# Uncast pixels, GpSimd adds and paired key jobs for the second batch of a spatial-reduction attention and GELU kernel

## The chip, the core and the metric

The kernel runs on one core of one Trainium2 chip. The metric is the device time of one launch in microseconds, the median of several runs; lower is better. The core has TensorE for matrix products (PE in the profile), ScalarE for activation functions (ACT), VectorE for elementwise work (DVE), GpSimd (POOL), and SyncE (SP), which here only issues transfers. Transfers run on 16 DMA engines. Products land in PSUM, which has eight banks of 128 x 512 float32.

## The reference

Two stages follow one another. Four batches of queries attend to keys that are a 4 x 4 average of an image, projected by one matrix; keys and values are the same. The result, 49152 rows of 128, goes through a feed-forward block of width 2048 with a sigmoid approximation of GELU.

```python
B, C, Hh, Ww = (4, 128, 384, 32)       # q: (4, 12288, 128), kv: (4, 384, 32, 128)
...
kv_pool = kv.reshape(B, H // r, r, W // r, r, C).mean(axis=(2, 4))   # r = 4
kv_flat = kv_pool.reshape(B, -1, C) @ w_sr                           # 768 keys a batch
k = v = kv_flat
s = scale * (q @ k.transpose(0, 2, 1))
s = s - s.max(-1, keepdims=True)
a = np.exp(s)
a /= a.sum(-1, keepdims=True) + 1e-09
return (a @ v).astype(np.float32)
...
h = x @ w_in                                                         # 128 -> 2048
g = h * (1.0 / (1.0 + np.exp(-1.702 * h)))
return (g @ w_out).astype(np.float32)                                # 2048 -> 128
```

## The kernel before

The work is cut into 96 groups of 512 rows. In attention a group has 6 chunks (128 keys by 512 rows), in the feed-forward block 16 chunks (128 hidden units by 512 rows). The program runs in two rounds: attention of groups 0 to 47, feed-forward of the same groups, then both again for groups 48 to 95. A Python scheduler in the kernel decides the order of all instructions while the program is built; each engine then takes its own instructions in that order.

One step of the main pipeline makes up to three chunks at once. TensorE fills three banks, and ScalarE turns them into bf16 in SBUF with one instruction, while the other three banks are filled:

```python
def fill_attn(chunks, ps):
    for k, (i, jc) in enumerate(chunks):
        rhs = qTs[i // 4][:, 0, (i % 4) * G:(i % 4 + 1) * G]
        nc.tensor.matmul(ps[:, k, :], kTs[i // GB][:, jc * 128:(jc + 1) * 128], rhs, start=True, stop=True)
    nc.scalar.activation(place([("a",) + c for c in chunks]), ps, AF.Exp, scale=scale)
...
def fill_moe(chunks, ps):
    ...
    nc.scalar.activation(place([("m",) + c for c in chunks]), ps, AF.Gelu_apprx_sigmoid)
```

Two banks (6 and 7) are left for everything else: the sums of values, the pooling, the keys. `acc()` hands them out in turn. A sum of values collects three tiles of 128 rows in one bank; VectorE then divides and writes the result to `x`, and the bank is free again:

```python
def drain_attn(t, a):
    ...
        nc.tensor.matmul(av_of[u][:, k * (C + 1):(k + 1) * (C + 1)], weights(("a", i, jc))[:, o:o + T],
                         vs[i // GB][:, jc, 0:C + 1], ...)
    ...
        nc.vector.reciprocal(rec, ps[:, :, C])
        ...
        nc.vector.tensor_tensor(to, ps[:, :, 0:C], rec.unsqueeze(2).broadcast_to([128, TS, C]), MUL)
```

The pixels of a batch are six chunks of 128 image half-rows. Those of the first two batches are loaded by a transfer that GpSimd issues and that turns float32 into bf16 on the way. TensorE adds four neighbours in a row by accumulating four products, and four neighbouring rows by its second operand `sum4`. A later job makes the keys and values of this chunk:

```python
def load_chunk(b, jc):
    a, ch = divmod(jc, HC)
    t = x_tile(XS - 1 - jc)
    nc.gpsimd.dma_start(out=t, in_=kv_r[b, a, ch])
    kv_tiles[b, jc] = t.rearrange("p (wp w1 c) -> p w1 wp c", w1=r, c=C)

def pool_chunk(b, jc):
    ps = acc()
    t = kv_tiles.pop((b, jc))
    for wp in range(4):
        for w in range(r):
            nc.tensor.matmul(ps[:, 32 * wp:32 * wp + 32], t[:, w, wp, :], sum4,
                             start=(w == 0), stop=(w == r - 1))
    pTs[b, jc] = kvtmp.tile([128, 128], BF, name="pTc", bufs=2)
    nc.vector.tensor_copy(pTs[b, jc], ps[:, 0:128])
...
def key_and_value(b, jc):
    ...
    nc.tensor.matmul(ps[:, 0:128], w_sr_sb, pTs[b, jc], start=True, stop=True)
    nc.tensor.matmul(ps[:, 128:256], pTs.pop((b, jc)), w_sr_sb, start=True, stop=True)
    nc.vector.tensor_copy(kTs[b][:, jc * 128:jc * 128 + 128], ps[:, 0:128])
    nc.vector.tensor_copy(vs[b][:, jc, 0:C], ps[:, 128:256])
```

`background(i)` starts the side work when group `i` of the attention begins. A gate (a one-element memset on VectorE, then one on GpSimd that waits for it) holds GpSimd's transfers back to that point; VectorE itself does not wait there:

```python
def background(i):
    ...
    if i in CAST:            # CAST = {0: [5], 13: [6], 14: [7], 15: [8], ...}: queries to bf16 in DRAM
        gate()
        for s in CAST[i]:
            cast_q(s)
    if i in (10, 12):
        gate()
        for jc in range(i % 10 * 3 // 2, i % 10 * 3 // 2 + 3):
            load_chunk(1, jc)
    if 0 <= i - 16 < JC:
        extras.append((key_and_value, 1, i - 16))
    if 0 <= i - 15 < JC:
        extras.append((pool_chunk, 1, i - 15))
```

Batch 1 is used from group 24 on. Some chunks are not ScalarE's: `early` and `rolling` exponentials and `lent` GELU chunks are made by VectorE with polynomials, a step at a time between its other work. A lent GELU chunk takes 15 VectorE instructions, two of them reciprocals of half a chunk.

Of the kernel before, what the change touches and what calls it, by code (L numbers as in the profile page):

```python
# [24 lines left out]
def kernel(  # L25
    ctx, tc, q, kv, w_sr, moe_w_in, moe_w_out, out,
):
    nc = tc.nc
    B, N, C = q.shape
    _, H, W, _ = kv.shape  # L30
    r = 4
    Hp, Wp = H // r, W // r
    J = Hp * Wp
    JC = J // 128
    d_ff = moe_w_in.shape[1]
    FCH = d_ff // 128
    scale = 1.0 / (C ** 0.5)
    G = 512
    SG = 4 * G
    NG = B * N // G  # L40
    NS = NG // 4
    GB = NG // B
# [10 lines left out]
    kv_r = kv.rearrange("b (ch p) (a w) c -> b a ch p (w c)", p=128, a=2)  # L53
# [6 lines left out]
    XS = NS // R  # L60
# [7 lines left out]
    kvtmp = ctx.enter_context(tc.tile_pool(name="kvtmp", bufs=1))  # L68
# [3 lines left out]
    opool = ctx.enter_context(tc.tile_pool(name="op", bufs=3))  # L72
# [43 lines left out]
    HC = H // 128  # L116
    h = J // 2
    kv_tiles, kv_sums, pooled, pTs, kTs, vs = {}, {}, {}, {}, {}, {}

    def new_keys(b):  # L120
        kTs[b] = kvres.tile([128, J], BF, name="kT")

        vs[b] = kvres.tile([128, JC, C + 8], BF, name="v")
        nc.vector.memset(vs[b][:, :, C:C + 1], 1.0)
# [16 lines left out]
        pTs[b, jc] = kvtmp.tile([128, 128], BF, name="pTc", bufs=2)  # L141
        nc.vector.tensor_copy(pTs[b, jc], ps[:, 0:128])

    def key_chunk(b, jc):
        if jc == 0:
            new_keys(b)
# [8 lines left out]
        vs[b, jc] = True  # L155

    def key_and_value(b, jc):
        if (b, jc) == (1, 0):
            new_keys(b)
        ps = acc()  # L160
        nc.tensor.matmul(ps[:, 0:128], w_sr_sb, pTs[b, jc], start=True, stop=True)
        nc.tensor.matmul(ps[:, 128:256], pTs.pop((b, jc)), w_sr_sb, start=True, stop=True)
        nc.vector.tensor_copy(kTs[b][:, jc * 128:jc * 128 + 128], ps[:, 0:128])  # L163
        nc.vector.tensor_copy(vs[b][:, jc, 0:C], ps[:, 128:256])
        vs[b, jc] = True
# [103 lines left out]
    for m in range(0, 128, 32):  # L269
        p = slice(m, m + 32)  # L270
# [3 lines left out]
    sum4 = cpool.tile([128, 32], BF)  # L274
# [3 lines left out]
    w_sr_sb = cpool.tile([128, C], BF)  # L278
# [40 lines left out]

    early = range(NG // R, NG // R + EARLY)  # L320
    rolling = [(i, JC - 1) for i in [*range(38, NG // R, 6), *range(57, 90, 6)]]
    lent = [(g, FCH - 1) for g in range(52, 94, 3)]
    aside = agpool.tile([128, K, 512], BF, name="aside")

    def weights(c):
# [112 lines left out]
    def lent_gelu(ps, out):  # L438
# [23 lines left out]
        for m in (0, 256):  # L462
            nc.vector.reciprocal(b[:, m:m + 256], a[:, m:m + 256])  # L463
            yield RECIPROCAL
        nc.vector.scalar_tensor_tensor(out, raw, -LN2 / 1.702, b, MUL, MUL)
# [21 lines left out]
    PART, FIRST = 24, 3  # L487

    def put_away(n, m):
        size = PART // 2 if n == 0 and m > FIRST else PART  # L490
        for o in range(m * PART, m * PART + PART, size):
            lo = n * XS * SG + o * T
            nc.sync.dma_start(out=x_bf[lo:lo + size * T, :].rearrange("(k p) c -> p k c", p=T),
                              in_=x[:, o * T:(o + size) * T].rearrange("p (k c) -> p k c", k=size))

    def bring_back(n, m):
        o = m * PART
        lo = n * XS * SG + o * T
        nc.sync.dma_start_transpose(out=x[:, o * T:(o + PART) * T].unsqueeze(1), in_=x_bf[lo:lo + PART * T, :])
# [6 lines left out]
    def gate():  # L506

        one = gate_tile[:, gates[0] % 8:gates[0] % 8 + 1]
        gates[0] += 1
        nc.vector.memset(one, 0.0)  # L510
        nc.gpsimd.memset(one, 0.0)  # L511

    TURN = {6: 3, 7: 4, 8: 5, 20: 6, 21: 7, 22: 8, 30: 9, 32: 10, 35: 11, 40: 12}
    CAST = {0: [5], 13: [6], 14: [7], 15: [8], 25: [9, 10], 26: [11, 12]}
    CAST_MOE = {20: 13, 21: 14, 22: 15, 23: 16, 33: 17, 34: 18, 35: 19, 36: 20, 37: 21, 38: 22, 39: 23}

    def background(i):

        first_round = i < GB * 2
        s = TURN.get(i, NS) if first_round else i // 4 + 3 if i % 4 == 0 else NS  # L520
        if s < NS:
            load_qT(s)
        if i in CAST:
            gate()
            for s in CAST[i]:
                cast_q(s)
        if i in (10, 12):
            gate()
            for jc in range(i % 10 * 3 // 2, i % 10 * 3 // 2 + 3):
                load_chunk(1, jc)  # L530
        if 0 <= i - 16 < JC:
            extras.append((key_and_value, 1, i - 16))
        if 0 <= i - 15 < JC:
            extras.append((pool_chunk, 1, i - 15))
        if i in (28, 33, 38):
            put_away(0, (i - 28) // 5)
        if i in (31, 36, 41):
            bring_back(0, (i - 31) // 5)
        if i == 27:
            gate()  # L540
            nc.gpsimd.dma_start(out=w_in_sb, in_=moe_w_in)
        if i == 28:
            gate()
            nc.gpsimd.dma_start(out=w_out_sb, in_=moe_w_out.rearrange("(o p) c -> p o c", p=128))
# [34 lines left out]
    extras = []  # L579
# [67 lines left out]
    for n in range(R):  # L647
        part = [c for c in chunks if c[0] // (NG // R) == n]
        while part:
            m = sizes.pop(0) if sizes else K  # L650
# [12 lines left out]
        while flat:  # L663
            m = K if len(flat) > sum(rest) else rest.pop(0)
# [25 lines left out]
    def jobs(p):  # L690

        nonlocal now
        for f, *args in first.get(p, ()):
            if f in COST:
                now = max(now, free[next_acc()])
            f(*args)
            if f in COST:
                now += COST[f][0]
                free[last_acc] = copied(f)

    def prepare(p):

        nonlocal now
        kind, part = seq[p]
        for i, jc in part:
            if (kind, i) not in begun:
                begun.add((kind, i))
                (background if kind == "a" else background_moe)(i)
            while kind == "a" and ((key_and_value, i // GB, jc) in extras or (transpose_q, i) in extras):
                f, *args = extras.pop(0)  # L710
                now = max(now, free[next_acc()]) + COST[f][0]
                f(*args)
                free[last_acc] = copied(f)
# [20 lines left out]


    FIXED, CHUNK, SWITCH, HANDOVER, EVACUATE = 0.295, 1.978, 6.0, 1.0, 4.5
    COST = {pool_chunk: (1.9, 2.6), key_chunk: (0.3, 2.4), value_chunk: (0.3, 2.4),
            transpose_q: (1.05, 4.2), early_fill: (1.0, 5.5), key_and_value: (0.55, 3.5),
            transpose_pooled: (0.9, 3.6), make_k: (0.8, 3.2), make_v: (0.8, 3.7)}
    COPY = {pool_chunk: 1.5, key_chunk: 1.5, value_chunk: 1.5, key_and_value: 2.8, transpose_q: 3.2}  # L740
    SMALL = 0.26
    RECIPROCAL = 10.5
    PAUSE = 4.0
    end, extra_at = [], 0.0
    source, dve = None, 0.0
# [2 lines left out]
    def on_dve(cost):  # L748
        nonlocal dve
        dve = max(dve, now + 1.0) + cost  # L750


    def copied(f):
        if f not in COPY:
            return now + COST[f][1]
        on_dve(COPY[f])
        return max(now + COST[f][1], dve)

# [28 lines left out]
    for n in range(len(seq)):  # L787
        fill(n + 2)
        jobs(n + 3)
        while True:  # L790
# [33 lines left out]
            kind, i, c = source[0]  # L824
# [58 lines left out]
```

The softmax here doesn't subtract the row's maximum and nothing guards it: scores larger than these inputs give would overflow.

## Time and profile before

| | |
|---|---|
| median of 3 runs | 950.75 us (950.52 to 951.18) |
| span of the profiled execution | 949.0 us |
| ScalarE busy | 933.9 us |
| TensorE busy | 941.5 us |
| VectorE busy | 536.8 us |
| GpSimd busy | 67.0 us |
| GELU instructions of ScalarE | 510, 682.2 us |
| exponential instructions of ScalarE | 192, 245.8 us |
| cast loads of pixels by GpSimd | 12 of 512 KB written, median 10.5 us from issue to landing |

A line of the groups names the line of the program, the engine, the operation, what is written and read with its shape, then the number of instructions; after the bar stand the busy time of the group in us, the mean ns of one instruction, and the idle time of the engine just before them with what ended most of it. A line of the timeline or of the chain of waits begins with the start in us from the start of the span and the duration in us. TensorE's matmuls are pipelined, so its busy time is not the same as its work. In the program before, L588 is the GELU, L342 the exponential, L340 the scores, L353 the sum of values, L139 the pooling, L376 and L379 the division of the attention's result, L130 the loads of pixels, and L510 the gate's memset on VectorE.

### The profile page before, as it was taken

The page shows a single profiled execution, that of the slowest core. Times are in us where ns is not written, and L with a number is a line of the kernel's source. Part 1 is how long each engine was busy: PE and PEld are TensorE (multiplying, and loading weights), DVE is VectorE, ACT ScalarE, POOL GpSimd, SP SyncE. Part 2 cuts the span into 40 slices and gives each one's busy share as a digit, 9 for nine tenths or more (in the row PEclk, how much of TensorE's full clock was granted, in tenths as well). Part 3 has the DMA queues.
Part 4 walks back from the last instruction along what each step waited for, and adds up shares of the span by engine and source line. Part 5 has one row for each costly group of instructions (what it writes and reads, how often), then busy time and mean ns, then how long its engine had stood idle before and what let it go on. Part 6 is the DMA issues. An engine that isn't in the chain of part 4 may idle for free.

```text
span 949.0 us, 15424 instructions
## 1 busy us (share of the span) xinstructions
PE 941.5 (99%) x6314; PEld 503.1 (53%) x6314; DVE 536.8 (57%) x1037; ACT 933.9 (98%) x708; POOL 67.0 (7%) x115
## 2 busy tenths in 40 slices
PE   8999999999999999999999999999999999999998
PEld 4677776444444444454446777754444444444444
DVE  5643553102477777778655765365666665566631
ACT  5999999999999999999999999999999999999998
POOL 4101001330000232000000000000000000000000
PEclk9999999999999999999999999999999999999999
DMA  9999922999867799865335583552222222222222
GB/s 182 203 181 193 214 57 42 157 127 170 162 132 113 116 147 125 123 103 78 65 55 112 133 160 77 134 122 35 44 34 45 34 46 34 45 33 45 34 45 45
DMA packets 372871, 94.93 MB, mean 100 GB/s; under 512 B 346736, under 2 KB 370416, under 8 KB 372464
## 3 DMA queue, kind: packets, MB, share of 16 engines
q1 hardware_dynamic: 343872, 61.31, 36.5%
q0 software_dynamic: 28656, 32.51, 22.6%
q8 instruction: 49, 0.80, 0.4%
q14 instruction: 22, 0.18, 0.1%
q10 hardware_dynamic: 272, 0.13, 0.0%
HBM read 52.49 MB, written 48.76 MB: 107 GB/s over the span
## 4 chain that ended last, share of the span: by engine, by line
ACT 88%; PE 9%; DMA 2%; issue 0%; DVE 0%; POOL 0%; POOLq 0%
ACT ag L588 71%; ACT ag L342 17%; PE banks L340 4%; PE banks L353 3%; DMA x<-in_kv_dram 1%; DMA qT<-q_bf 1%; PE banks L139 0%; PE banks L586 0%; PE banks L624 0%; ACT L588 0%; PE banks L596 0%; PE banks L233 0%; ACT L342 0%; DVE kT L163 0%; POOL x L222 0%
## 5 line engine op out<-in xcount | busy, mean ns | idle before, releaser
L588 ACT ACTIVATE ag<-banks 128x1536 bf16<-128x1536 f32 (+1 forms) x510 | 682.2, 1507 | 0.0
L586 PE MATMUL banks<-x,w_in_sb 128*128 128x512 bf16 x1522 | 411.7, 379 | 0.1
L596 PE MATMUL banks<-ag,w_out_sb 128*128 128x512 bf16 x1506 | 407.8, 379 | 0.0
L342 ACT ACTIVATE ag<-banks 128x1536 bf16<-128x1536 f32 (+2 forms) x192 | 245.8, 1439 | 3.7 <-PE banks L340 3.3
L596 PEld LDWEIGHTS <-w_out_sb 128*128 128x128 bf16 x1520 | 148.5, 98 | 178.0 <-issue 0.9
L586 PEld LDWEIGHTS <-w_in_sb 128*128 128x128 bf16 x1522 | 147.3, 98 | 170.4 <-issue 1.1
L607 DVE STREAM_TRANSPOSE o_sb<-banks 128x512 f32<-128x512 f32 x95 | 67.9, 715 | 210.7 <-PE banks L596 199.9
L353 PEld LDWEIGHTS <-ag 128*128 128x128 bf16 x2272 | 146.1, 98 | 46.4 <-issue 0.6
L353 PE MATMUL banks<-v,ag 128*128 128x129 bf16 x2272 | 163.7, 220 | 0.1
L340 PE MATMUL banks<-qT,kT 128*128 128x512 bf16 x544 | 148.7, 379 | 1.6 <-DVE kT L163 1.0
L432 DVE SCALAR_TENSOR_TENSOR ea<-ea,eb 128x512 f32<-128x512 f32 x128 | 87.8, 686 | 3.2
L376 DVE RECIPROCAL rec<-banks 128x3 f32<-128x3 f32 x124 | 22.2, 179 | 96.0 <-PE banks L353 96.0
L379 DVE TENSOR_TENSOR x<-banks,rec 128x384 bf16<-128x384 f32 x124 | 69.1, 557 | 4.3
L340 PEld LDWEIGHTS <-kT 128*128 128x128 bf16 x544 | 46.3, 98 | 26.6 <-DVE kT L163 1.7
L463 DVE RECIPROCAL eb<-ea 128x256 f32<-128x256 f32 x28 | 47.6, 1726 | 0.5
L173 POOL DMA_DIRECT2D kvs<-in_kv_dram x32 | 40.4, 1315 | 20.8 <-DMA kvs<-in_kv_dram 17.8
L421 DVE TENSOR_SCALAR ea<-banks 128x512 f32<-128x512 f32 x32 | 22.1, 692 | 32.6 <-PE banks L405 32.4
L456 DVE SCALAR_TENSOR_TENSOR ea<-ea,eb 128x512 f32<-128x512 f32 x56 | 38.3, 685 | 1.6
L511 POOL MEMSET gate_tile<- 1x1 f32 x37 | 3.9, 105 | 323.1 <-DVE gate_tile L510 323.1
L427 DVE SCALAR_TENSOR_TENSOR eb<-eb,ea 128x512 f32<-128x512 f32 x32 | 22.1, 690 | 0.9
L443 DVE TENSOR_SCALAR qT<-banks 128x512 f32<-128x512 f32 x14 | 9.7, 692 | 17.2 <-PE banks L399 16.9
L434 DVE SCALAR_TENSOR_TENSOR ag<-ea,ee 128x512 bf16<-128x512 f32 x24 | 16.5, 688 | 0.7
(84 smaller groups left out, 267.6 us busy)
## 6 DMA issues: line engine op xcount, KB each, us to landing
out_dram<-o_sb SPq DMA_DIRECT2D x380, 64.0 KB, 2.0
kvs<-in_kv_dram POOLq DMA_DIRECT2D x32, 384.0 KB, 6.5
q_bf<-in_q_dram POOLq DMA_DIRECT2D x21, 512.0 KB, 6.9
x_bf<-x SPq DMA_DIRECT2D x12, 768.0 KB, 5.8
x<-in_kv_dram POOLq DMA_DIRECT2D x12, 512.0 KB, 10.5
x_bf<-x SPq DMA_DIRECT2D x8, 384.0 KB, 4.5
x<-in_q_dram POOLq DMA_DIRECT2D x5, 256.0 KB, 15.2
w_in_sb<-in_moe_w_in_dram POOLq DMA_DIRECT2D x1, 512.0 KB, 9.6
```

Source lines behind the costliest of these rows:

```text
L173: nc.gpsimd.dma_start(out=kv_sums[b][:, i2], in_=kv_p[b, i, w, :, i2], **({"accum_op": ADD} if n else {}))
L340: nc.tensor.matmul(ps[:, k, :], kTs[i // GB][:, jc * 128:(jc + 1) * 128], rhs, start=True, stop=True)
L342: nc.scalar.activation(place([("a",) + c for c in chunks]), ps, AF.Exp, scale=scale)
L353: nc.tensor.matmul(av_of[u][:, k * (C + 1):(k + 1) * (C + 1)], weights(("a", i, jc))[:, o:o + T], vs[i // GB][:, jc, 0:C + 1], start=(jc = ...
L379: nc.vector.tensor_tensor(to, ps[:, :, 0:C], rec.unsqueeze(2).broadcast_to([128, TS, C]), MUL)
L432: nc.vector.scalar_tensor_tensor(a, a, COEFFS[k], b, ADD, MUL)
L456: nc.vector.scalar_tensor_tensor(a, a, COEFFS[k], b, ADD, MUL)
L463: nc.vector.reciprocal(b[:, m:m + 256], a[:, m:m + 256])
L586: nc.tensor.matmul(ps[:, k, :], w_in_sb[:, fc * 128:(fc + 1) * 128], x[:, g % (4 * XS) * G:(g % (4 * XS) + 1) * G], start=True, stop=True)
L588: nc.scalar.activation(place([("m",) + c for c in chunks]), ps, AF.Gelu_apprx_sigmoid)
L596: nc.tensor.matmul(o_of[g], w_out_sb[:, fc, :], weights(("m", g, fc)), start=(fc == 0), stop=(fc == FCH - 1))
L607: nc.vector.transpose(o_sb, o_of.pop(g))
```

## The change

Four things are changed, nearly all for batch 1.

1. Its pixels are loaded as float32 by SyncE, without a cast, into three spaces of twice the size; loads 3 to 5 use the spaces of loads 0 to 2 again. A one-element memset on VectorE goes ahead of each load.
2. GpSimd adds the four neighbours in a row with three additions and writes bf16. TensorE then adds only the four rows: 8 narrow products for two chunks in place of 32.
3. Pooling and keys are jobs of two chunks each, so three of each in place of six.
4. VectorE makes 17 GELU chunks in place of 14; the scheduler's own estimate of a reciprocal is made smaller to match. The casts of queries 6 to 8 begin at groups 16 to 18 in place of 13 to 15, and one write of results to DRAM is cut in two.

The aim is to take work off TensorE and ScalarE in the first attention block and in the last feed-forward block.

```diff
+    def load_pixels(jc):
+        a, ch = divmod(jc, HC)
+        o = (XS - JC) * SG + jc % 3 * 2 * SG
+        t = x[:, o:o + 2 * SG].bitcast(F32)
+        nc.vector.memset(t[:, 0:1], 0.0)
+        nc.sync.dma_start(out=t, in_=kv_r[1, a, ch])
+        kv_tiles[1, jc] = t.rearrange("p (wp w1 c) -> p w1 wp c", w1=r, c=C)
+
+    def sum_pixels(jc):
+        t = kv_tiles.pop((1, jc))
+        if jc % 2 == 0:
+            held[jc // 2] = opool.tile([128, 512], F32, name="o_sb").bitcast(BF)
+        sums[jc] = held[jc // 2][:, jc % 2 * 512:jc % 2 * 512 + 512].rearrange("p (wp c) -> p wp c", c=C)
+        nc.gpsimd.tensor_tensor(t[:, 0], t[:, 0], t[:, 1], ADD)
+        nc.gpsimd.tensor_tensor(t[:, 2], t[:, 2], t[:, 3], ADD)
+        nc.gpsimd.tensor_tensor(sums[jc], t[:, 0], t[:, 2], ADD)
+
+    def pool_sums(b, jc):
+        ps = acc()
+        for k in range(2):
+            for wp in range(4):
+                o = k * 128 + 32 * wp
+                nc.tensor.matmul(ps[:, o:o + 32], sums[jc + k][:, wp, :], sum4, start=True, stop=True)
+        pTs[b, jc] = kvtmp.tile([128, 256], BF, name="pTp")
+        nc.vector.tensor_copy(pTs[b, jc], ps[:, 0:256])
+
+    def key_pair(b, jc):
+        ...
+        nc.tensor.matmul(ps[:, 0:256], w_sr_sb, pT, start=True, stop=True)
+        for k in range(2):
+            nc.tensor.matmul(ps[:, 256 + k * 128:384 + k * 128], pT[:, k * 128:(k + 1) * 128], w_sr_sb,
+                             start=True, stop=True)
+        nc.vector.tensor_copy(kTs[b][:, jc * 128:(jc + 2) * 128], ps[:, 0:256])
+        nc.vector.tensor_copy(vs[b][:, jc:jc + 2, 0:C], ps[:, 256:512].rearrange("p (k c) -> p k c", k=2))
...
-    lent = [(g, FCH - 1) for g in range(52, 94, 3)]
+    lent = [(g, FCH - 1) for g in range(52, 94) if g % 5 in (2, 4)]
...
-        size = PART // 2 if n == 0 and m > FIRST else PART
+        size = PART // 2 if n == 0 and m > 1 else PART
...
-    CAST = {0: [5], 13: [6], 14: [7], 15: [8], 25: [9, 10], 26: [11, 12]}
+    CAST = {0: [5], 16: [6], 17: [7], 18: [8], 25: [9, 10], 26: [11, 12]}
...
-        if i in (10, 12):
-            gate()
-            for jc in range(i % 10 * 3 // 2, i % 10 * 3 // 2 + 3):
-                load_chunk(1, jc)
-        if 0 <= i - 16 < JC:
-            extras.append((key_and_value, 1, i - 16))
-        if 0 <= i - 15 < JC:
-            extras.append((pool_chunk, 1, i - 15))
+        if 10 <= i < 10 + JC:
+            if i > 10:
+                sum_pixels(i - 11)
+            for jc in range(3) if i == 10 else [i - 8] if i < 14 and i > 10 else []:
+                load_pixels(jc)
+        if i == 10 + JC:
+            sum_pixels(JC - 1)
+        if i in range(15, 15 + JC, 2):
+            extras.append((pool_sums, 1, i - 15))
+        if i in range(16, 16 + JC, 2):
+            extras.append((key_pair, 1, i - 16))
...
-    RECIPROCAL = 10.5
+    RECIPROCAL = 8.2
```

More of the change, by code (lines that the diff above doesn't have):

```diff
@@ L142, in pool_chunk @@
         nc.vector.tensor_copy(pTs[b, jc], ps[:, 0:128])
+    held, sums = {}, {}
+    def load_pixels(jc):
[22 more added lines that the diff above has]
+    def key_pair(b, jc):
+        if jc == 0:
+            new_keys(b)
+        ps = acc()
+        pT = pTs.pop((b, jc))
+        nc.tensor.matmul(ps[:, 0:256], w_sr_sb, pT, start=True, stop=True)
[4 more added lines that the diff above has]
+        nc.vector.tensor_copy(vs[b][:, jc:jc + 2, 0:C], ps[:, 256:512].rearrange("p (k c) -> p k c", k=2))
+        vs[b, jc] = vs[b, jc + 1] = True
     def key_chunk(b, jc):
@@ L157, in key_and_value @@
     def key_and_value(b, jc):
-        if (b, jc) == (1, 0):
-            new_keys(b)
         ps = acc()
@@ L708, in prepare @@
                 (background if kind == "a" else background_moe)(i)
-            while kind == "a" and ((key_and_value, i // GB, jc) in extras or (transpose_q, i) in extras):
+            while kind == "a" and ((key_pair, i // GB, jc // 2 * 2) in extras or (transpose_q, i) in extras):
                 f, *args = extras.pop(0)
@@ L736 @@
     FIXED, CHUNK, SWITCH, HANDOVER, EVACUATE = 0.295, 1.978, 6.0, 1.0, 4.5
-    COST = {pool_chunk: (1.9, 2.6), key_chunk: (0.3, 2.4), value_chunk: (0.3, 2.4),
+    COST = {pool_chunk: (1.9, 2.6), pool_sums: (1.1, 3.2), key_pair: (1.1, 5.0), key_chunk: (0.3, 2.4), value_chunk: (0.3, 2.4),
             transpose_q: (1.05, 4.2), early_fill: (1.0, 5.5), key_and_value: (0.55, 3.5),
             transpose_pooled: (0.9, 3.6), make_k: (0.8, 3.2), make_v: (0.8, 3.7)}
-    COPY = {pool_chunk: 1.5, key_chunk: 1.5, value_chunk: 1.5, key_and_value: 2.8, transpose_q: 3.2}
+    COPY = {pool_chunk: 1.5, pool_sums: 2.1, key_pair: 4.2, key_chunk: 1.5, value_chunk: 1.5, key_and_value: 2.8, transpose_q: 3.2}
     SMALL = 0.26
-    RECIPROCAL = 10.5
+    RECIPROCAL = 8.2
     PAUSE = 4.0
```

## The prediction

> **What bounds the kernel now.** I read four views, in this order: the engine totals, the costliest groups, the chain of waits, and then the timelines of the stage that the change touches (38 to 76 us, the second half of the first attention block).
>
> ```profile
> PE 941.5 (99%) x6314; PEld 503.1 (53%) x6314; DVE 536.8 (57%) x1037; ACT 933.9 (98%) x708; POOL 67.0 (7%) x115
> ...
> ACT 88%; PE 9%; DMA 2%; issue 0%; DVE 0%; POOL 0%; POOLq 0%
> ...
> L588 ACT ACTIVATE ag<-banks 128x1536 bf16<-128x1536 f32 (+1 forms) x510 | 682.2, 1507 | 0.0
> ...
> L342 ACT ACTIVATE ag<-banks 128x1536 bf16<-128x1536 f32 (+2 forms) x192 | 245.8, 1439 | 3.7 <-PE banks L340 3.3
> ```
>
> The reader is to see that ScalarE (ACT) has 0.0 us of idle time before its 510 GELU instructions and 3.7 us before its 192 exponentials. Everything after the first 13 us is one unbroken row of ScalarE instructions. So time leaves this kernel only if ScalarE gets fewer instructions, and any interval in which ScalarE goes dry is added to the end in full. The pitch of one three-chunk instruction, from the chain of waits in the last stretch:
>
> ```profile
> 885.54 37.63 ACT ag L588 x28
> ```
>
> 37.63 / 28 = 1.344 us. In the first attention block TensorE (PE) is level with ScalarE. There the chain, cut to 40 to 50 us, runs through TensorE alone:
>
> ```profile
> 42.64 0.65 PE banks L340 x3
> 43.28 0.68 PE banks L353 x12
> 43.96 0.65 PE banks L340 x3
> 44.61 0.68 PE banks L353 x12
> 45.29 0.65 PE banks L340 x3
> ```
>
> Three score matmuls and twelve value matmuls take 0.65 + 0.68 = 1.33 us, against ScalarE's 1.344: each exponential starts as soon as its three score matmuls end, so a wait of TensorE reaches ScalarE after about one instruction. VectorE's (DVE) timeline of the same stretch shows who hands the accumulation banks back to TensorE:
>
> ```profile
> 40.67 0.18 DVE L376 RECIPROCAL rec<-banks 128x3 f32<-128x3 f32 x1 [2.26 <-PE banks L353]
> 40.88 0.56 DVE L379 TENSOR_TENSOR x<-banks,rec 128x384 bf16<-128x384 f32 x1
> 42.33 0.18 DVE L376 RECIPROCAL rec<-banks 128x3 f32<-128x3 f32 x1 [0.90 <-PE banks L353]
> 42.55 0.56 DVE L379 TENSOR_TENSOR x<-banks,rec 128x384 bf16<-128x384 f32 x1
> 44.00 0.18 DVE L376 RECIPROCAL rec<-banks 128x3 f32<-128x3 f32 x1 [0.90 <-PE banks L353]
> 44.22 0.56 DVE L379 TENSOR_TENSOR x<-banks,rec 128x384 bf16<-128x384 f32 x1
> 44.71 0.06 DVE L510 MEMSET gate_tile<- 1x1 f32 x1
> ```
>
> Every value group (three tiles of 128 rows) ends in a reciprocal and a multiply, 0.78 us from start to end, and only two banks take turns in this stage. The memset at 44.71 is a gate: in the kernel before it waits for nothing.
>
> [...]No run here shows a GpSimd add.[...] The trace before has the cast loads of the second batch: issued at 39.0, 39.6 and 40.1 us, 7.0, 9.0 and 11.1 us to landing, so about 2.5 us apart, each reading 1 MB and writing half of it.[...] VectorE's order therefore decides what is behind a wait. The trace agrees: its timeline keeps program order.
>
> **The change part by part.**
>
> 1. *Three more GELU chunks on VectorE* (14 to 17). 754 chunks of the second half become 751, exactly one three-chunk ScalarE instruction fewer: 510 to 509. Gain 1.34 us, in full. VectorE's price: a chunk is 0.69 + 4 x 0.43 + 0.69 + 4 x 0.69 + 0.69 + 0.42 + 2 x 1.73 + 0.67 = about 11.1 us by the mean durations of its groups, so 33 us more in a block of 338 us (604 to 942) in which VectorE is busy 192 us. A lent chunk now comes every 2 or 3 groups; one group of 16 chunks takes 16/3 x 1.344 = 7.2 us, so the shorter distance is 14.3 us. It fits.
>
> 2. *Pooling on TensorE.* Before: 16 narrow matmuls per chunk, 0.39 to 0.43 us in the chain (the first reads "52.92 0.43", others 0.39), six times: 2.4 us. After: 8 per pair, 24 instead of 96, about 0.6 us. Keys and values: before two matmuls of 128 columns, 0.12 to 0.15 us, six times, some 0.75; after one of 256 and two of 128 columns, about 0.22, three times, 0.65. TensorE loses 1.9 us of work. But ScalarE has almost no gap there to give back: its only visible one is 0.11 us (busy 1.89 of 2.00 at 60 to 62 us), and its late starts after pool matmuls sum to about 0.3 us. Gain 0.3 us.
>
> 3. *Loads uncast through SyncE, adds on GpSimd, memsets on VectorE.* The DMA now writes 1 MB a chunk. Since the cast load already read 1 MB in 2.5 us, I take 2.5 to 3.5 us a chunk. The cost is in the order. On VectorE, the memset ahead of load 3 follows the evacuation at 40.67; by the order of instructions it waits for GpSimd's sum of chunk 0, whose space load 3 reuses. Two evacuations later the memset of load 4 waits for sum 1, one evacuation after that the memset of load 5 waits for sum 2.
>
>    When is sum 0 done? SyncE issues load 0 behind its third query transpose, which the trace has at 37.76 for 2.13 us, so at 39.9. Landing: 5.7 us later, about 45.6 (the first cast load needed 7.0 beside the transpose[...]). Sum 0 ends at 45.6 + 3.6 = 49.2. VectorE reaches the memset at 41.4 and stands until 49.2.
>
>    TensorE at 44.61 wants the bank that the evacuation of 42.33 frees. That now ends at 49.2 + 0.85 = 50.05. Then 0.68 of value matmuls, 0.65 of score matmuls, and the exponential that started at 46.01 starts at 51.4. **First stall: 5.4 us.**
>
>    Sum 1 ends 3.6 us after sum 0. VectorE has by then done both held evacuations; TensorE's next need of a bank is 4.8 us after sum 0, the evacuation behind memset 4 ends at 3.6 + 0.85 = 4.45. No stall. Sum 2 ends at 7.2; the next bank is needed at 6.45 and free at 7.2 + 0.85 = 8.05. **Second stall: 1.6 us.**
>
>    Later: sums 3, 4 and 5 end at 10.8, 14.4 and about 18.5 us after sum 0 (two cast issues lie between). With both stalls, TensorE reaches the three pairs' pooling at about 11, 16 and 22 us after sum 0 and needs sums 1, 3 and 5 there: no wait, with 3 us to spare at the last.
>
> 4. *Casts of queries moved from groups 13-15 to 16-18, smaller pieces written out, pairs of keys.* The casts now stand behind sum 4 and sum 5 in GpSimd's queue. Relative to the shifted work they land within about 3 us of before, and their transposes were issued at 66 us or later for groups from 24 on (after 75 us). I count zero.
>
> Sum: 950.75 - 1.34 - 0.3 + 5.4 + 1.6 = 956.1. I choose 955.6, a little lower, because only errors in the order could make the stalls vanish and the time then falls to one point.
>
> **Rivals.**
>
> *No stall*: if the memsets found GpSimd done, the gains would stand alone: 950.75 - 1.64 = 949.1. For it speaks that the change thins TensorE and ScalarE at once, and that VectorE is busy only 57%. Against it: a load of 1 MB issued at 39.9 and three adds cannot be over by 43.8, the last moment at which the first stall is zero by the above.
>
> *GpSimd becomes the bound of the stage*: with 4.5 us a sum instead of 3.6 the stalls are 6.3 and 3.4 us, and sum 5 would come about 1.4 us after TensorE wants it. That makes 960. A higher price for each add[...] would do this.[...]
>
> *VectorE becomes a bound in the last block* with its 17 chunks: a bank handed back late, or a value matmul waiting for its lent chunk. The profile speaks against it: 192 + 33 = 225 of 338 us busy.
>
> **Range and chances.** Adds of 1.0 to 1.4 us and a landing of 44.5 to 47 us move the stalls between about 4 and 11 us in all: 953 to 960. I widen the low end to 951.5 for a stall partly hidden by exponentials already prepared. Two per cent is 19 us: none of the paths reaches it in either direction. Faster 0.01, same 0.97, slower 0.02. That it is slower than before at all I hold for 85% likely.
>
> **What would show it.** The changed profile should have 509 GELU instructions; an idle time before the exponentials of some 9 to 11 us in place of 3.7; memsets of the pixel space on VectorE preceded by idle time put down to GpSimd, about 8 us at 41 us and some 3 us at the third; GpSimd adds of 1.0 to 1.4 us; and no idle time before pooling matmuls for the second or third pair. If the exponentials show no such idle time near 46 us, my reading of VectorE's order is wrong; if pooling waits for GpSimd, the price of an add is.

## The result and the profile after

| | before | after |
|---|---|---|
| median of six runs of each | 951.01 us (950.52 to 952.17) | 961.58 us (960.42 to 963.70) |
| ratio, 95% interval | | 1.0110 (1.0097 to 1.0123) |
| span of the profiled execution | 949.0 us | 957.5 us |

The change makes the kernel 1.1% slower, 10.6 us. The prediction was 955.6 us with a range up to 960.0. It had the sign and most of the place; the loss is about twice as large as predicted. The profiled execution is one of the shorter ones (spans of the six timed runs: 957.5 to 960.5 us); runs 10 and 11 below come back to that. Ledgers of microseconds below are in spans.

From the page of the changed kernel, the totals, the chain's shares and the two groups of ScalarE:

```profile
PE 941.7 (98%) x6239; PEld 502.2 (52%) x6239; DVE 567.0 (59%) x1077; ACT 933.0 (97%) x707; POOL 85.4 (9%) x125
...
PE 50%; ACT 46%; DMA 2%; issue 1%; DVE 0%; POOL 0%; SPq 0%; DVEq 0%; POOLq 0%
...
L633 ACT ACTIVATE ag<-banks 128x1536 bf16<-128x1536 f32 (+1 forms) x509 | 680.9, 1503 | 0.1
...
L384 ACT ACTIVATE ag<-banks 128x1536 bf16<-128x1536 f32 (+2 forms) x192 | 246.0, 1435 | 13.7 <-PE banks L382 13.4
```

ScalarE has one GELU instruction fewer, as planned (509), and its idle time before the exponentials has gone from 3.7 to 13.7 us, ended by TensorE's scores. Its busy time is nearly unchanged, so everything lost is in those waits. The view of waits names what TensorE and VectorE were waiting for (microseconds in total, times, the longest):

```profile
ACT ag L384 <- PE banks L382: 13.4, 5, 6.9
DVE rec L418 <- issue: 8.0, 1, 8.0
PE banks L395 <- DVE x L421: 5.7, 1, 5.7
...
DVE x L151 <- POOL o_sb L163: 2.4, 1, 2.4
PE banks L447 <- DMA qT<-q_bf: 2.2, 1, 2.2
```

One stand of VectorE of 8.0 us, one of TensorE of 5.7 us, and, much later, one of 2.2 us for a query transpose. The first, on VectorE's timeline (start, duration, what, and in brackets the idle time ahead):

```profile
40.84 0.56 DVE L421 TENSOR_TENSOR x<-banks,rec 128x384 bf16<-128x384 f32 x1
49.43 0.17 DVE L418 RECIPROCAL rec<-banks 128x3 f32<-128x3 f32 x1 [8.04 <-issue]
49.45 0.06 DVE L151 MEMSET x<- 128x1 f32 x1
...
53.23 0.06 DVE L151 MEMSET x<- 128x1 f32 x1 [2.36 <-POOL o_sb L163]
```

and on GpSimd's timeline:

```profile
45.58 1.26 POOL L161 TENSOR_TENSOR x<-x 128x512 f32<-128x512 f32 x1 [26.91 <-DMA x<-in_kv_dram]
46.80 1.25 POOL L162 TENSOR_TENSOR x<-x 128x512 f32<-128x512 f32 x1
48.13 1.26 POOL L163 TENSOR_TENSOR o_sb<-x 128x512 bf16<-128x512 f32 x1
49.35 1.26 POOL L161 TENSOR_TENSOR x<-x 128x512 f32<-128x512 f32 x1
```

The third add of chunk 0 ends at 48.13 + 1.26 = 49.39, and VectorE's memset of the space that this chunk held runs at 49.45. The page puts the 8.04 us down to "issue", and shows the reciprocal a hair ahead of the memset, as their records overlap; the order of the program and the end of the add tell what it was. What it did to TensorE:

```profile
43.76 0.81 PE L382 MATMUL banks<-qT,kT 128*128 128x512 bf16 x3
50.25 1.46 PE L395 MATMUL banks<-v,ag 128*128 128x129 bf16 x12 [5.68 <-DVE x L421]
51.50 1.48 PE L382 MATMUL banks<-qT,kT 128*128 128x512 bf16 x3
52.78 1.50 PE L395 MATMUL banks<-v,ag 128*128 128x129 bf16 x12
54.08 1.38 PE L382 MATMUL banks<-qT,kT 128*128 128x512 bf16 x3
```

After the stand, the starts are 1.25 to 1.30 us apart where they were about 0.65. The stretches of the same trace (limits, length, busy time of PE, PEld, DVE, ACT and POOL with instructions, then the granted clock, the DMA share and GB/s) say why:

```profile
43.80:48.40 4.60, 0.77 (x6) 0.25 (x4) 0.00 (x0) 2.32 (x2) 2.75 (x3) 1.00 1.01 422
48.40:50.20 1.80, 0.00 (x0) 0.00 (x0) 0.73 (x4) 0.00 (x0) 1.80 (x2) 0.50 0.43 182
50.20:52.80 2.60, 2.55 (x16) 1.71 (x16) 0.64 (x2) 0.00 (x0) 2.52 (x3) 0.50 0.87 246
52.80:55.20 2.40, 2.40 (x16) 1.73 (x15) 0.80 (x3) 1.45 (x1) 2.40 (x3) 0.50 0.79 229
```

TensorE's granted clock is 0.50 from 48.4 us on, while it still stands, and stays so until 55.2. Last, the third wait in the chain:

```profile
101.40 8.72 DMA qT<-q_bf
110.12 0.05 issue
110.17 0.39 PE banks L447
```

The transpose of queries 9 is issued at 101.40 us and takes 8.72 us to land. In the kernel before it took 7.41 us, and its wait was 0.2 us; from the chain of the kernel before:

```profile
93.04 7.41 DMA qT<-q_bf
```

Adding up the distances between the ends of successive ScalarE instructions above the ordinary pitch gives the ledger of this trace: first stall +7.0, second +1.1 (at 57 us), third +2.3 at 113 us against 0.2 in the kernel before, one GELU triple less 1.3, and a tail behind the last GELU that is 0.4 shorter (1.58 to 1.16). 949.0 + 7.0 + 1.1 + 2.1 - 1.3 - 0.4 = 957.5.

### The profile page after: what moved, and what is told of

Its sections match the earlier page's. It is cut to its first block, busy times and chain, and to the rows that moved or that the text cites. A ratio compares the mean times of both kernels' runs of the same rounds, so it can differ in the third digit from the quotient of the medians.

```text
span 957.5 us, 15350 instructions
## 1 busy us (share of the span) xinstructions
PE 941.7 (98%) x6239; PEld 502.2 (52%) x6239; DVE 567.0 (59%) x1077; ACT 933.0 (97%) x707; POOL 85.4 (9%) x125
## 4 chain that ended last, share of the span: by engine, by line
PE 50%; ACT 46%; DMA 2%; issue 1%; DVE 0%; POOL 0%; SPq 0%; DVEq 0%; POOLq 0%
ACT ag L633 34%; PE banks L631 18%; PE banks L641 17%; ACT ag L384 12%; PE banks L395 7%; PE banks L382 6%; DMA x<-in_kv_dram 1%; DMA qT<-q_bf 1%; PE banks L447 1%; PE banks L669 0%; PE banks L139 0%; PE banks L275 0%; ACT L633 0%; DVE kT L205 0%; POOL x L264 0%
## 5 line engine op out<-in xcount | busy, mean ns | idle before, releaser
L384 ACT ACTIVATE ag<-banks 128x1536 bf16<-128x1536 f32 (+2 forms) x192 | 246.0, 1435 | 13.7 <-PE banks L382 13.4
L474 DVE SCALAR_TENSOR_TENSOR ea<-ea,eb 128x512 f32<-128x512 f32 x128 | 87.5, 684 | 3.8 <-DVE ea L474 0.6
L505 DVE RECIPROCAL eb<-ea 128x256 f32<-128x256 f32 x34 | 57.8, 1724 | 0.5
L498 DVE SCALAR_TENSOR_TENSOR ea<-ea,eb 128x512 f32<-128x512 f32 x68 | 46.6, 686 | 2.0
L485 DVE TENSOR_SCALAR qT<-banks 128x512 f32<-128x512 f32 x17 | 11.7, 691 | 22.9 <-PE banks L441 22.6
```

The costliest lines, as they stand in the source:

```text
L474: nc.vector.scalar_tensor_tensor(a, a, COEFFS[k], b, ADD, MUL)
L498: nc.vector.scalar_tensor_tensor(a, a, COEFFS[k], b, ADD, MUL)
```

## The experiments

The theory was: the loss is made by waits on the way loads, GpSimd, VectorE's memset, bank, TensorE, and not by more work; take the waits away and the change gains. Rivals: GpSimd or the transfers simply can't deliver in time; the gain of the lent chunks isn't there; or the half clock, and not the waits, is the greater part. Each edit is against the changed kernel unless said otherwise.

| run | median us (range) | ratio to before, 95% | span |
|---|---|---|---|
| 1 memsets on GpSimd | 960.83 (960.43 to 961.64) | 1.0099 (1.0085 to 1.0113) | 959.4 |
| 2 TensorE kept busy | 957.95 (957.47 to 958.15) | 1.0067 (1.0053 to 1.0081) | 956.3 |
| 3 lent chunks alone | 951.31 (950.72 to 952.02) | 0.9998 (0.9990 to 1.0006) | 949.4 |
| 4 run 1, pooling later | 961.26 (960.68 to 964.51) | 1.0113 (1.0095 to 1.0132) | 958.5 |
| 5 run 4, query casts as before | 957.16 (955.13 to 958.57) | 1.0061 (1.0049 to 1.0074) | 954.9 |
| 6 run 5, query transpose 9 earlier | 957.53 (954.80 to 961.14) | 1.0068 (1.0048 to 1.0088) | 953.0 |
| 7 run 6, 14 lent chunks | 958.62 (956.00 to 961.77) | 1.0080 (1.0061 to 1.0099) | 954.0 |
| 8 run 5, pixels earlier, weights later | 950.71 (949.37 to 951.80) | 0.9994 (0.9985 to 1.0002) | 949.0 |
| 9 run 8, query casts behind the loads | 949.27 (949.07 to 951.19) | 0.9981 (0.9974 to 0.9988) | 947.3 |

### Run 1: the memsets of loads 3 to 5 on GpSimd

```diff
-        nc.vector.memset(t[:, 0:1], 0.0)
+        (nc.vector if jc < 3 else nc.gpsimd).memset(t[:, 0:1], 0.0)
```

GpSimd's own order now keeps the memset behind the sum (the third add of chunk 0 ends at 47.98 + 1.27 = 49.25, the memset runs at 49.31); VectorE waits for nothing here.

> The memsets ahead of loads 3 to 5 go from VectorE to GpSimd; all else and TensorE's order stay. Theory A (VectorE standing at its memset is the cause, but GpSimd's chain of sums comes next): the 8 us wait of VectorE goes and the clock stays at 1.0, but TensorE then reaches pooling of the second pair at about 58.2 us and finds sum 3 at 60.7, and of the third pair at about 66 and finds sum 5 at 68.9: two waits of 2.5 and 2.8 us on GpSimd, together 5.2 in place of 8.1, so about 958.6 us. Theory B (the memset is the whole cost of the stage): about 953.4 us, no waits at pooling. Theory C (late pixels, not the memset): no change, 961 us, with VectorE's wait gone but the same idle time on ScalarE.

VectorE's 8.0 us are gone, and the time is the same. TensorE's timeline in this run:

```profile
57.67 0.81 PE L382 MATMUL banks<-qT,kT 128*128 128x512 bf16 x3
58.35 0.25 PE L171 MATMUL banks<-sum,o_sb 128*128 128x32 bf16 x4
61.25 0.27 PE L171 MATMUL banks<-sum,o_sb 128*128 128x32 bf16 x4 [2.65 <-POOL o_sb L163]
...
62.65 1.50 PE L395 MATMUL banks<-v,ag 128*128 128x129 bf16 x12
63.95 1.48 PE L382 MATMUL banks<-qT,kT 128*128 128x512 bf16 x3
```

The first pooling products of the second pair are made and the next four wait 2.65 us for GpSimd's sum: without the stall TensorE comes too early for sums that are 3.8 us apart. The granted clock is 0.50 from 62.4 to 65.8 us behind this shorter wait also; ScalarE loses 3.0 + 1.2 + 0.3 + 0.9 us between 60 and 71 us. The rest went to the third wait, 4.9 us here and 6.3 us for ScalarE. So VectorE's memset was one of two gates in series: the stall that it made had hidden GpSimd's.

### Run 2: TensorE kept busy while it waits

24 products of 512 columns into a bank that is about to be filled anyway, at the place where TensorE stands; they compute nothing that is used.

```diff
+        if t == 24 and a == 0:
+            for _ in range(24):
+                nc.tensor.matmul(banks[:32, K * ((filled + 1) % 2), :], ones,
+                                 ones.unsqueeze(1).broadcast_to([128, 16, 32]), start=True, stop=True)
...
```

`filled` is the number of the step that was filled last; the lines that keep it are left out here.

> 24 idle matmuls (about 5.2 us, results unused, into the bank that is filled next) are put where TensorE waits for VectorE. Theory A (TensorE's standing still halves its clock for 6.8 us): the clock stays at 1.0, ScalarE's first idle time falls from 6.9 to about 5.5 us, the second stays at 1 to 1.9 us but now as a wait for the bank behind the third memset; about 960.6 us. Rival (the halved clock has another cause, or costs nothing that the waits don't hide): 961.6 us and a clock of 0.5 in the same place.

```profile
44.84 5.34 PE L393 MATMUL banks<-ones 128*32 128x512 bf16 x24 [0.26 <-ACT ag L384]
50.73 0.84 PE L399 MATMUL banks<-v,ag 128*128 128x129 bf16 x12 [0.56 <-DVE x L425]
...
58.32 0.50 PE L399 MATMUL banks<-v,ag 128*128 128x129 bf16 x6 [1.77 <-DVE x L425]
```

and a stretch of this run, in the columns as above:

```profile
44.50:50.50 6.00, 5.42 (x25) 2.41 (x25) 0.55 (x3) 1.63 (x2) 4.38 (x4) 1.00 0.75 315
```

The clock stays at 1.00, where the changed kernel has 0.50 from 48.4 us on: with TensorE kept busy it isn't halved here. The median is 961.58 - 957.95 = 3.6 us less than that of the changed kernel, with the wait of VectorE left as it was. The first stall is 6.2 us in place of 7.0, though the first sum, and with it the bank, came 0.5 us later; the bank is free 0.56 us after the idle products end. And now a second stall shows at 58.32: TensorE waits 1.77 us for the bank behind the memset of load 5. This is the second stall of the prediction, as it was predicted. It costs ScalarE 1.9 us, so the two stalls come to 8.1 us, as in the changed kernel (7.0 + 1.1). In the changed kernel the wait didn't occur, since the half clock had slowed TensorE by about as much:

```profile
55.69 1.27 POOL L163 TENSOR_TENSOR o_sb<-x 128x512 bf16<-128x512 f32 x1
...
57.21 0.56 DVE L421 TENSOR_TENSOR x<-banks,rec 128x384 bf16<-128x384 f32 x1
...
57.96 0.84 PE L395 MATMUL banks<-v,ag 128*128 128x129 bf16 x12
```

The bank is free at 57.77 and wanted in the middle of these twelve products, at about 58.3. This 0.5 us, an estimate, is what the half clock cost the changed kernel here; the rest of its slow products lay in time that TensorE would have waited for GpSimd's third sum anyway. The two traces are only 1.2 us apart (957.5 and 956.3), and that is the third wait, 1.0 us of ScalarE's idle time in this run and 2.2 in the changed kernel; why it is shorter here isn't shown. What makes up the rest of the 3.6 us isn't shown; run 11 shows one thing that it can be.

### Run 3: the lent chunks alone, in the kernel before

```diff
-    lent = [(g, FCH - 1) for g in range(52, 94, 3)]
+    lent = [(g, FCH - 1) for g in range(52, 94) if g % 5 in (2, 4)]
...
-    RECIPROCAL = 10.5
+    RECIPROCAL = 8.2
```

> The kernel before with only the 17 GELU chunks on VectorE and the scheduler's smaller estimate of a reciprocal. Theory: one ScalarE instruction less, 1.34 us, so 949.6 us, ratio 0.9986. Rival (VectorE hands banks back late in the last block and takes the gain): 950.5 to 952 us.

Nothing is gained: a gain of 1.34 us would be a ratio of 0.9986, which the interval leaves out. ScalarE's last GELU ends 1.15 us earlier (942.95 for 944.10), but the end isn't ScalarE's. TensorE's last products, first in the kernel before, then in this run:

```profile
942.76 3.07 PE L624 MATMUL banks<-w_out_sb,ag 128*128 128x128 bf16 x52
```

```profile
943.00 3.23 PE L624 MATMUL banks<-w_out_sb,ag 128*128 128x128 bf16 x55 [0.31 <-DVE o_sb L607]
```

TensorE has the same products to make whoever makes the GELU, and finishes no earlier. Of the 0.4 us by which it ends later here, 0.31 is a wait for VectorE, so the rival of a bank handed back late has a part. That a chunk less on ScalarE pays once work is taken off TensorE too, as part 2 of the change does, is a conclusion that no run isolates; run 7 comes back to it.

### Runs 4 to 7: following the waits downstream

Run 4 is run 1 with pooling and keys three groups later, so that GpSimd's sums are ready.

```diff
-        if i in range(15, 15 + JC, 2):
-            extras.append((pool_sums, 1, i - 15))
-        if i in range(16, 16 + JC, 2):
-            extras.append((key_pair, 1, i - 16))
+        if i in range(18, 18 + JC, 2):
+            extras.append((pool_sums, 1, i - 18))
+        if i in range(19, 19 + JC, 2):
+            extras.append((key_pair, 1, i - 19))
```

> The gate on GpSimd as in the first run, and pooling and keys begun three groups later (18, 20, 22 and 19, 21, 23), about 8 us, so that every sum is there before it is asked for. Theory A: no idle time of ScalarE between 40 and 75 us; 951.3 us if the wait for the ninth query transpose near 100 us stays at 2.2 us, 949.4 us if it goes back to 0.2. Rival (GpSimd's adds hold up VectorE or TensorE in another way): 953 us or more.

From 40 to 76 us no wait is left, and the time is no better. TensorE's timeline:

```profile
80.52 0.38 PE L382 MATMUL banks<-qT,kT 128*128 128x512 bf16 x1 [4.16 <-DMA qT<-q_bf]
```

The queries of batch 1 aren't there. Their cast stands behind the sums in GpSimd's queue: it was issued at 65.3 us, the transpose behind it at 70.7, landing at 80.5. In the changed kernel the stalls had given it that time. ScalarE loses 5.7 us here and 5.0 at the wait for queries 9, with half clock behind both: the products behind three score products start 1.27 and 1.28 us after them, for 0.65 (at 82.69 and 111.70 us).

Run 5 puts the casts of queries 6 to 8 back to where the kernel before has them.

```diff
-    CAST = {0: [5], 16: [6], 17: [7], 18: [8], 25: [9, 10], 26: [11, 12]}
+    CAST = {0: [5], 13: [6], 14: [7], 15: [8], 25: [9, 10], 26: [11, 12]}
```

> As the fourth run (gate on GpSimd, pooling three groups later), with the casts of queries 6 to 8 back at groups 13 to 15, so that they stand between the sums in GpSimd's queue and not behind them. Theory A (in the fourth run the queries of group 24 came late because their casts stood behind the sums): the 5.7 us of idle time of ScalarE at 81 to 87 us go; the wait for query transpose 9 at 105 us falls to between 0.2 and 3 us. 949 to 953 us. Rival (transposes are late because the uncast loads and the casts share the DMA engines, wherever the casts stand): 956 us or more, with idle time again near 80 us.

```profile
74.49 0.27 PE L171 MATMUL banks<-sum,o_sb 128*128 128x32 bf16 x4 [3.12 <-POOL o_sb L163]
...
104.96 0.39 PE L447 MATMUL banks<-qT,kT 128*128 128x512 bf16 x1 [2.25 <-DMA qT<-q_bf]
```

That is 4.1 us better (961.26 to 957.16). The wait for queries at 80 us is gone, but the last pixel load, issued at 58.5 us, takes until 70.5 beside the casts, and the last sum is late. Run 6 issues the query transpose behind the wait at 105 us two groups earlier:

```diff
-    TURN = {6: 3, 7: 4, 8: 5, 20: 6, 21: 7, 22: 8, 30: 9, 32: 10, 35: 11, 40: 12}
+    TURN = {6: 3, 7: 4, 8: 5, 20: 6, 21: 7, 22: 8, 28: 9, 32: 10, 35: 11, 40: 12}
```

> As the fifth run, with query transpose 9 issued at group 28 in place of 30. Theory A: the last wait near 105 us goes, ScalarE has no gap over 0.2 us after the first 15 us, and the 17 GELU chunks count because TensorE has lost 1.9 us of pooling: 948.5 to 949.5 us, below both kernels. Rival (the earlier transpose meets the casts of groups 25 and 26 and the weights, and lands no earlier, or a later transpose is late instead): the same as the fifth run or slower.

A miss: it is issued at 89.6 us, lands at 105.0 all the same, 15 us later, and TensorE's wait is 3.4 us. The casts of groups 25 and 26 and the loads of weights of groups 27 and 28 stand beside it in the program; its own earlier issue brought nothing. Run 7 is run 6 with 14 lent chunks:

```diff
-    lent = [(g, FCH - 1) for g in range(52, 94) if g % 5 in (2, 4)]
+    lent = [(g, FCH - 1) for g in range(52, 94, 3)]
...
-    RECIPROCAL = 8.2
+    RECIPROCAL = 10.5
```

> As the sixth run, but with the 14 GELU chunks and the larger estimate of a reciprocal of the kernel before: the change to the pixels alone, without its waits. Theory A (TensorE and ScalarE are both full, so neither part pays alone): 950.0 to 950.8 us, about 0.5 us below before, and 1.3 us above the sixth run. Rival (TensorE's lost work is worth its 1.9 us): 949 us; or the waits are still there: 952 us or more.

Its median is 1.1 us above run 6, in the direction of one ScalarE instruction more, but the two intervals overlap: inconclusive. The two traces are 1.0 us apart, 0.6 of it in the wait for the last sum, so only 0.4 us is left for the lent chunks. The waits of TensorE at 74 and 105 us are there as in run 6 (2.6 and 3.4 us; 2.0 and 3.4 in run 6), so VectorE's three more chunks don't make them.

### Runs 8 and 9: all the waits taken away

Run 8 is run 5 with the first three pixel loads four groups earlier, and the loads of the feed-forward weights, which stood beside query transpose 9, at groups 36 and 38.

```diff
-        if 10 <= i < 10 + JC:
-            if i > 10:
-                sum_pixels(i - 11)
-            for jc in range(3) if i == 10 else [i - 8] if i < 14 and i > 10 else []:
-                load_pixels(jc)
+        if i == 6:
+            for jc in range(3):
+                load_pixels(jc)
+        if 10 < i < 10 + JC:
+            sum_pixels(i - 11)
+            if i < 14:
+                load_pixels(i - 8)
...
-        if i == 27:
+        if i == 36:
             gate()
...
-        if i == 28:
+        if i == 38:
             gate()
```

> As the fifth run, with the first three pixel loads issued at group 6, ahead of two query transposes, and the two weight loads moved from groups 27 and 28 to 36 and 38, out of the way of query transpose 9. Theory A (what is left of the loss is transfers that come late: the last pixels, and query transpose 9 behind casts and weights): the sums end about 5 us earlier, the wait at 71 us and the wait at 105 us go, ScalarE has no gap over 0.3 us after the first 15 us: 948.5 to 949.5 us, below both kernels. Rival (TensorE and the DMA engines are full over the whole block and a wait only moves): another wait of 2 us or more takes their place, 953 us or more.

The wait for query transpose 9 is gone, so the weights had most likely been what held it up: run 8 moved the pixel loads too, but those had landed by 65.7 us. One wait is left, on TensorE's timeline:

```profile
72.84 0.27 PE L171 MATMUL banks<-sum,o_sb 128*128 128x32 bf16 x4 [1.26 <-POOL o_sb L163]
```

The last pixel load was issued at 53.0 us and landed at 65.7, beside the casts of queries 6 and 7. The time is that of the kernel before, 1 to 2 us above what was expected. Run 9 lets the casts wait for the loads:

```diff
-    CAST = {0: [5], 13: [6], 14: [7], 15: [8], 25: [9, 10], 26: [11, 12]}
+    CAST = {0: [5], 15: [6], 16: [7], 17: [8], 25: [9, 10], 26: [11, 12]}
```

> As the run before it, only the casts of queries 6 to 8 begin two groups later (15 to 17 in place of 13 to 15), behind sum 3 in GpSimd's queue, so that pixel loads 3 to 5 no longer share the transfers with casts 6 and 7. Theory (the last wait is that sharing): load 3, issued at 48.4 us, lands near 55 in place of 60.7, sum 5 ends near 66 in place of 72.8, the 1.26 us of ScalarE near 75.6 us vanish, transpose 6 still lands before 76; span 947.7, time about 949.4, ratio 0.998. Rival (the casts now come too late, as in the run with later pooling alone): transpose 6 lands after 78, TensorE stands for the scores of group 24, its clock may halve: 952 to 955.

From its page, totals, shares of the chain and the two groups of ScalarE:

```profile
PE 940.3 (99%) x6239; PEld 500.8 (53%) x6239; DVE 567.5 (60%) x1074; ACT 932.3 (98%) x707; POOL 86.1 (9%) x128
...
PE 98%; DMA 1%; ACT 0%; POOL 0%; DVE 0%; issue 0%; POOLq 0%
...
L635 ACT ACTIVATE ag<-banks 128x1536 bf16<-128x1536 f32 (+1 forms) x509 | 680.9, 1511 | 0.0
...
L384 ACT ACTIVATE ag<-banks 128x1536 bf16<-128x1536 f32 (+2 forms) x192 | 245.4, 1479 | 3.5 <-PE banks L382 3.2
```

Load 3 lands at 55.2 us in place of 60.7, the last sum ends at 67.8 in place of 72.8, and no ScalarE gap above 0.12 us is left between 28 us and the last GELU. The median is 949.27 us, 2.0 us below the kernel before measured beside it (951.28): faster than both kernels, by 0.2% against the kernel before. The exponentials' idle time is back at 3.5 us, and the chain now runs 98% through TensorE.

### Runs 10 and 11: the changed kernel twice more

No edit.

> The changed kernel once more, nothing edited, for the spread of its spans: six timed runs list spans of 957.5, 957.5, 959.9, 960.5, 959.7 and 959.8 us, and the profile that was read is of 957.5. Theory (the waits for transfers vary, and the profile read is a fortunate one): a trace of about 959.8 us, in which the third wait, for the query transpose before 110 us, is 4 to 5 us in place of 2.2, or is long enough to halve TensorE's clock once more; stalls one and two stay at 7.0 and 1.1 within 0.3. Rival (the first stall varies[...]): stall one or two 2 us longer, the third wait the same.

> The same kernel a third time, for the same question: a span between 957.3 and 960.6 us, and the differences between the three traces in the third wait alone (theory) or in the first two stalls (rival).

Spans of 957.8 and 960.0 us. Run 10 repeats the ledger of the first trace to 0.3 us (7.2, 0.9, 2.4). Run 11, TensorE's timeline at the third wait:

```profile
110.96 0.52 PE L447 MATMUL banks<-qT,kT 128*128 128x512 bf16 x1 [2.21 <-DMA qT<-q_bf]
111.27 1.18 PE L395 MATMUL banks<-v,ag 128*128 128x129 bf16 x9
```

The third wait is not longer, 2.21 us for 2.22, but this time it costs a half clock of about 3.4 us: ScalarE loses 3.6 + 0.4 us there, not 2.3. That is 1.6 of the 2.5 us between the two traces; the other 0.8 are in the first two stalls (7.5 + 1.2 + 0.3). Each theory has part of it. Most of the difference between these traces comes from whether a wait of 2.2 us brings the clock down.

What stretches of the two traces show there, in the columns as above, first the first trace, then run 11:

```profile
107.00:110.00 3.00, 0.95 (x9) 0.34 (x6) 0.56 (x2) 2.52 (x2) 0.00 (x0) 1.00 1.24 150
110.00:113.00 3.00, 2.83 (x31) 2.01 (x32) 2.09 (x5) 1.25 (x1) 0.00 (x0) 1.00 1.16 243
113.00:117.00 4.00, 4.00 (x49) 2.94 (x47) 3.11 (x8) 4.00 (x4) 0.00 (x0) 1.00 1.22 277
```

```profile
110.00:110.90 0.90, 0.00 (x0) 0.00 (x0) 0.00 (x0) 0.32 (x1) 0.00 (x0) 1.00 0.45 97
110.90:112.00 1.10, 1.04 (x8) 0.84 (x9) 0.48 (x1) 0.00 (x0) 0.00 (x0) 0.59 1.28 290
112.00:114.00 2.00, 2.00 (x13) 1.18 (x11) 1.65 (x5) 0.23 (x1) 0.00 (x0) 0.50 1.18 212
114.00:114.40 0.40, 0.40 (x7) 0.40 (x6) 0.06 (x1) 0.40 (x1) 0.00 (x0) 0.50 1.28 291
114.40:118.00 3.60, 3.55 (x39) 2.54 (x39) 1.76 (x5) 3.29 (x3) 0.00 (x0) 0.99 1.19 276
```

In the first trace the granted clock stays at 1.00 through the wait and behind it. In run 11 it comes down as the wait ends: 0.59 over 1.10 us puts the fall at about 111.1, and 0.99 over the last 3.60 us the return at about 114.5, an estimate of 3.4 us at half clock. Why the same wait does so in one trace and not in the other isn't shown.

## Why the prediction fell short

**What bounds the first attention block, the order on VectorE, the way to the bank:** right. The memset stood 8.04 us, as predicted about 8; its cause is shown by run 1, which took it away alone.

**Part 1, one ScalarE instruction less, "Gain 1.34 us, in full":** not right as a gain of its own. Run 3 shows that alone it brings nothing, because TensorE is as full as ScalarE at the end. In the ledger of the whole change 1.3 and 0.4 us of tail stand against the 1.34 + 0.3 of the sum; how much of it the lent chunks bring isn't shown (runs 6 and 7). The rival *no stall* had 949.1 us for the change without its waits, 1.64 less than before; run 9, which is that with its loads and casts moved, has 949.27, 2.0 less than the kernel before beside it. That the two agree so closely is in part luck.

**Part 3, the loads and the adds:** right. The first load landed at 45.4 us (predicted about 45.6), the next two 2.5 us apart; an add took 1.26 us, a sum 3.8 us. The 3.6 us of the prediction for a sum was its author's estimate; the trace of the kernel before has no add on GpSimd.

**Part 3, "First stall: 5.4 us":** the mechanism right, the size off; it was 7.0 to 7.5. The failed term is "0.68 of value matmuls, 0.65 of score matmuls" behind the stand, which were priced at the full clock. They took 1.25 and 1.28 us, 1.2 us more, and the bank was free 0.15 us later than predicted. The prediction let TensorE stand for over 5 us without asking what its clock does then. In the first trace it was idle from 44.57 us, half clock began 3.8 us into that, at 48.4, and lasted 6.8 us. In run 1 it lasted 3.4 us behind a wait of 2.65, in run 11 about 3.4 behind one of 2.21.

**Part 3, "Second stall: 1.6 us":** about the size (1.1), not for the stated reason. In the changed kernel it is the half clock; the wait for the bank that was predicted appears only in run 2, where the clock is kept up, with 1.77 us. Taken together the two stalls were 8.1 us against 7.0. About 0.5 of the difference is the half clock's own (run 2); 0.6 is the third sum, which ended at 56.96 us where the prediction's terms give 49.2 + 7.2 = 56.4, as a sum took 3.8 and not 3.6 us and the first ended 0.2 later.

**Part 4, "I count zero":** wrong, and the larger part of the miss: 2.1 us in one trace, 3.8 in another, 1.6 of this by half clock. I compared the transposes of queries 6 to 8 with the groups that use them and left those further on out. The transpose of queries 9 had been just in time in the kernel before (a wait of 0.2 us). After the change it was issued 8.4 us later while TensorE wanted it 7.7 us later (7.66), and took 1.3 us longer to land: 0.7 + 1.3 = 2.0. In run 8, with the weights out of its way, the wait is gone. The moved casts aren't the cause, since run 5 with the casts put back still waits 2.25 us. Why it took 1.3 us longer in the changed kernel isn't settled.

In sum: predicted -1.64 + 5.4 + 1.6 = +5.4 us, of which the 955.6 takes 4.9. The trace of 957.5: -1.7 + 7.0 + 1.1 + 2.1 = +8.5. That of 960.0: -1.8 + 7.5 + 1.5 + 3.8 = +11.0. The medians differ by 10.6. So two steps failed: the count of zero for the later transposes, worth 2.1 to 3.8 us, and the size of the two stalls, 8.1 to 9.0 us in place of 7.0. The line of the prediction "what would show it" with its 9 to 11 us of idle time before the exponentials saw 13.7.

**The rival "GpSimd becomes the bound of the stage"** is refuted in its price of 4.5 us a sum, yet there is something in it: the third sum sets the end of the two stalls (run 2), and with the memset out of the way (run 1) TensorE waited for sums, 2.65 us at one. Taken alone, the sums are 6 x 3.8 = 23 us, and they fit in as soon as the loads come earlier (run 9). An add took 1.25 to 1.28 us in the changed kernel, whether VectorE stood (45 to 49 us) or worked, so nothing is seen of a wait for VectorE.

## What to carry to other kernels

Where two engines are full together, a wait that TensorE takes for a few microseconds costs its length and can cost a stretch at half clock (7.0 us of ScalarE for a wait of 5.68 in the first trace). Price the products behind such a stand at double (1.25 to 1.30 us here for 0.65), then ask whether a later wait would have taken that time anyway: here it took most of it. A gate belongs on the engine that has made the space free, not on one that hands out banks to others; and before work is put on an otherwise idle engine, list everything that stands behind it in that queue and behind its transfers, down to those that were just in time. When removing one wait brings nothing, the next in series has been uncovered: follow it until the trace has none, before judging the change.

## What the runs showed of the hardware that was not expected

- The clock came down behind waits of TensorE of 2.65 us (run 1) and 2.21 us (run 11), while a wait of 2.22 us in the first trace left it at 1.00 (107 to 117 us), and waits of 3.1 us (run 5) and 3.4 us (runs 6 and 7) did not bring it down either: the products behind that of run 5 start 0.65 us apart, and the mean over the whole traces of runs 6 and 7 is 1.000. So the length of a wait alone doesn't tell; what does isn't shown. The half clock lasted 3.4 us behind those of runs 1 and 11, and 6.8 behind the stand of 5.7 us in the first trace.
- A transfer that reads float32 pixels and writes them uncast was no slower than one that casts: landings about 2.5 us apart for 1 MB read each in both kernels (46.0, 48.6 and 51.2 us before, 45.4, 47.9 and 50.4 in the changed one), in the changed one at 422 GB/s (43.8 to 48.4 us).
- The transpose of queries 9 took from 5.4 us (run 9, issued at 93.1, landed at 98.4) to 15 us (run 6, issued at 89.6, landed at 105.0) to land. In run 9 the loads of weights had been moved away from it.
